# Reordering a planned kernel: new due times and transfer rules for a Fourier filter followed by a gated convolution

## Chip, cores and metric

The kernel runs on one NeuronCore of a Trainium2 chip. The metric is the device time of one execution in microseconds (us); the median of several executions counts. The engines are named as in the profile: PE is TensorE (matrix products), PEld its weight loads, DVE is VectorE, ACT is ScalarE, POOL is GpSimd, SP is SyncE, which here issues nearly all DMA transfers. SPq is SP's queue.

## What is computed

The input x has 8 batches of 3200 positions with 256 channels. Each batch is Fourier transformed along its positions, mixed by a complex matrix, soft-thresholded, and transformed back; a causal convolution of the result over five positions then gates a linear map of it, and a second linear map follows.

```python
X = np.fft.rfft(x, axis=1)
Yr = Xr @ w_r - Xi @ w_i + b_r
Yi = Xr @ w_i + Xi @ w_r + b_i
Yr = np.sign(Yr) * np.maximum(np.abs(Yr) - 0.01, 0.0)   # Yi likewise
y = np.fft.irfft(Yr + 1j * Yi, n=3200, axis=1)
gate_pre = sum(conv_w[k] * shifted(y, k) for k in range(5))
out = (sigmoid(gate_pre) * (y @ w_val)) @ w_out
```

## The kernel before

The transform of length 3200 = 64 x 50 is done in two stages, so that each batch goes through three parts.

**P1** (`p1`, and `p1_first` for batch 0): in 8 pieces a batch, x is loaded (two transfers of 200 KB), PE multiplies it with the 50-point transform f1 (tile p, line 499), ACT copies the result to s, and SP stores it to a buffer in HBM, a_dram.

**P2** (`p2`): in 13 steps u a batch, two frequency groups each (one in the last). SP loads a from a_dram. PE transforms it over 64 points with f2 (tile s, line 538, called s2 in the code). ACT and DVE split s into a high and a low half, xs (lines 548 and 550), and ACT adds a negated copy (553). PE mixes with w_r and w_i in y_ps, 12 products for each group (lines 573 and 574). DVE adds the bias (yb, 589), ACT and DVE do the threshold (tp, 594 and 596), both split the result into r_hl (293 and 295), and PE transforms it back over 64 points in z_ps (621). ACT copies that to z_t, which SP stores to z_dram.

**P3** (`positions` and `gated`): in 8 blocks k a batch, SP loads zl from z_dram, PE makes the inverse 50-point transform y_p (675), ACT copies it to y_sb. From y_sb come the product with w_val in v_ps (707, from a split y_hl; 703 for late blocks, from y_sb and the unsplit weights w_late) and the convolution: one ACT step (733) and four taps for each half of the channels on DVE (acc, 736), eight taps a block. ACT applies the sigmoid (746), DVE multiplies by v_ps (748) and splits the product (gated, 295), PE multiplies by w_out in o_ps (707), ACT copies it to o, and SP writes it out.

Before the first P3 of batch 0, DVE converts w_val, conv_w and w_out from 64-bit floating point (`from_float64`, lines 321 and 327: 13 steps for each matrix).

The three parts of neighbouring batches overlap: while batch b is in P2, batch b+1 is in P1 and batch b-1 in P3. What stands where is not written out by hand. Every piece of work is given to the class `Plan` by `add`, with a due time `at`, an engine, an estimated duration and the tiles that it uses and makes. `at` is counted in steps of P2 (13 a batch), shifted by the table `O`. `Plan.order` then walks through a model of the engines: on each, of the pieces that could begin within `SLACK` ns of the first, it takes the one with the lowest due time; it keeps one estimate, `wire`, of when the DMA engines are free; and it adds `LAND` ns after a piece before another engine may use its result. `SWITCH` prices a change on PE between the products of P1 and of y_p, which use a quarter of the array each (`quarters`), and the others. The kernel's instructions are issued in the order that results, each engine's in its own row; on the chip an engine takes its row strictly in that order, and only dependences set the time. `SLOTS` limits the buffers: one PSUM tile for each of s, y_ps and z_ps, two for p, y_p, v_ps and o_ps together, three buffers of x, a and zl.

The last two batches use some cheaper forms (`LATE_VAL`, `LATE_OUT`, `LATE_P2`): without a split, in full 32-bit products, which take PE longer and DVE and ACT shorter.

Of the kernel before, what the change touches and what calls it, by code (L numbers as in the profile page):

```python
# [79 lines left out]
class Plan:  # L80
# [30 lines left out]
    def order(self):  # L111
# [24 lines left out]
        free = {e: 0.0 for e in engines}  # L136
        in_quarters, wire = False, 0.0
# [13 lines left out]
        while len(done) < len(pieces):  # L151
            best = None
            for e in engines:
                could = []
                for p in waiting[e]:
                    at = opens(p)
                    if at is not None:
                        could.append((max(free[e], p["ready"], at), p))
                if not could:
                    continue  # L160
                first = min(c[0] for c in could)
                near = [c for c in could if c[0] <= first + SLACK[e]]
                start, p = min(near, key=lambda c: (c[1]["at"] - (TOGETHER if e == "PE" and in_quarters and c[1]["quarters"] else 0.0), c[0]))
                if best is None or start < best[0]:
                    best = start, p
            assert best is not None, "no piece can begin"
            start, p = best
            e = p["engine"]
            waiting[e].remove(p)
            busy, delay = p["busy"], p["delay"]  # L170
            if e == "PE":
                slow = max([f for until, f in CLOCK if start < until], default=1.0)
                busy, delay = busy * slow, delay * slow
                if in_quarters != p["quarters"]:
                    busy, delay = busy + SWITCH, delay + SWITCH
                in_quarters = p["quarters"]
            if p["kb"]:
                wire = max(wire, start + 800) + p["kb"] * 1024 / WIRE
                delay = wire - start + 1400
            free[e] = start + busy  # L180
            end = start + delay
            p["start"], p["end"] = start, end
            done.append(p)
            for t, tag in p["new"].items():
                rows[tag].append(t)
            for t in p["tiles"]:
                if t in users:
                    users[t] -= 1
                    ends[t] = max(ends[t], end)
            for n, at in [(n, end) for n in after[p["n"]]] + [(n, start) for n in follow[p["n"]]]:  # L190
                q = pieces[n]
                q["left"] -= 1
                q["ready"] = max(q["ready"], at)
                if not q["left"]:
                    waiting[q["engine"]].append(q)
# [22 lines left out]
def act(n, kind="copy"):  # L218
# [3 lines left out]

NU = (NT + 1) // 2
T = float(NU)
O = {
    "load_x": -1.5, "p1": -0.28, "p1_step": 1.25, "load_a": -2.0, "s2": -0.6, "s1i": 0.4,
    "p3": 2.6, "load_z": -2.0, "y": 0.2, "conv": 0.3, "val": 0.5, "gate": 0.9, "project": 1.2,
}
# [5 lines left out]

LATE = [(b, k) for b in (B - 2, B - 1) for k in range(NB)]
LATE_P2 = {(B - 1, NU - 2)}
LATE_VAL = set(LATE[5:])
LATE_OUT = set(LATE[15:])


@with_exitstack
def fourier_filter_then_gated_conv(ctx: ExitStack, tc: tile.TileContext, x, w_r, w_i, b_r, b_i,
# [3 lines left out]
    sb = ctx.enter_context(tc.tile_pool(name="sb", bufs=2))  # L246
    ps = ctx.enter_context(tc.tile_pool(name="ps", bufs=1, space=bass.MemoryType.PSUM))
    dram = ctx.enter_context(tc.tile_pool(name="dram", bufs=2, space=bass.MemoryType.DRAM))
    plan = Plan(SLOTS)
    add = plan.add  # L250
    tl = {}
# [233 lines left out]
    def p1(b, u, at):  # L485
# [20 lines left out]
        def store():  # L506
# [4 lines left out]
            for k in range(2):  # L511
                lo = u * 4 * D + k * 512
                nc.sync.dma_start(out=dst[:, :, lo:lo + 512], in_=st[k * HP:k * HP + N2])
        add(at + O["load_x"] + (b == 1), "SP", 700, load, STORED if b == 1 else (), [kx + (0,)], {kx: "x"}, kb=400, chain="x")
# [5 lines left out]
    def p2(b, u, at):  # L520
# [16 lines left out]
            for c in range(2):  # L537
                nc.tensor.matmul(p[:, 2 * i + c, :], tl[ka][:, i, c * P:(c + 1) * P], f2_sb[:, t, :], start=True, stop=True)  # L538
# [65 lines left out]
        kz, ko, kd = ("z_ps", bu), ("z_t", bu), ("z_dram", b)  # L604
# [46 lines left out]
    def positions(b, k, at):  # L651
# [28 lines left out]
        add(at, "PE", 900, s2i, [kz + (0,), ("g2", 0, 0), *free], [kp + (0,)], {kp: "ps_2"}, quarters=True, chain="s2i")  # L680
# [146 lines left out]

    def p1_all(b):
        for u in range(8):
            p1(b, u, (b - 1) * T + O["p1"] + u * O["p1_step"])  # L830
    for b in range(B):
        if b < B - 1:
            p1_all(b + 1)
# [8 lines left out]
        start = (b + 1) * T + O["p3"]  # L842
# [31 lines left out]
```

## Time and profile before

| | before |
|---|---|
| three runs | 994.38, 990.14, 991.02 us; median 991.02 us |
| profiled execution | 995.47 us, span 993.7 us |
| mean granted clock of TensorE | 0.963 |
| instructions | 23846, of them 9918 matmuls on PE |
| moved by DMA | 164.53 MB, mean 166 GB/s |

The span is the time from the first to the last instruction; the profiled execution's own time is 1.8 us longer. Busy time of PE counts the time in which at least one matmul is in flight. A full 32-bit product of the program appears as two records of matmul in the profile (256 rows of p in the program are 512 records). A row of the chain of waits has a start, a duration and what it was.

### The profile page before, as it was taken

What the parts mean: (1) busy time and instruction counts of PE and PEld (TensorE: products, weight loads), DVE (VectorE), ACT (ScalarE), POOL (GpSimd) and SP (SyncE); (2) the same over time, 40 slices, a digit from 0 to 9 for tenths busy, and PEclk for the clock granted to TensorE, in tenths of its full rate; (3) what the DMA queues carried; (4) which work ended last, traced back from release to release, by engine and by line L of the source; (5) the groups of instructions that cost most, each with busy time, mean ns of one, the idle gap of its engine ahead of it and who ended that gap; (6) DMA issues with size and microseconds to landing.
All of it is one profiled execution on the core that took longest, in us unless ns stands there. A gap on an engine that the chain in (4) does not pass through costs nothing.

```text
span 993.7 us, 23846 instructions
## 1 busy us (share of the span) xinstructions
PE 928.2 (93%) x9918; PEld 822.0 (83%) x9918; DVE 745.3 (75%) x1211; ACT 671.8 (68%) x1091; POOL 3.7 (0%) x8
## 2 busy tenths in 40 slices
PE   7699779999999999999999999999999899998896
PEld 2477648999898988899989998998988899996664
DVE  1244655979678886888797897889777798897775
ACT  1265446777677787678787787768686777775554
POOL 0000000000000000000000000000000000000000
PEclk8799959999999999999999999999999999999799
DMA  6688466443665357544665366635655245323321
GB/s 213 212 266 266 134 186 205 135 126 125 217 201 190 120 154 268 189 150 130 222 203 173 120 212 217 205 115 163 205 184 174 67 135 184 103 92 105 122 67 67
DMA packets 105233, 164.53 MB, mean 166 GB/s; under 512 B 10054, under 2 KB 78406, under 8 KB 105126
## 3 DMA queue, kind: packets, MB, share of 16 engines
q1 hardware_dynamic: 104166, 159.74, 50.3%
q10 hardware_dynamic: 960, 3.28, 0.9%
q8 instruction: 78, 1.28, 0.5%
q14 instruction: 29, 0.24, 0.1%
HBM read 84.34 MB, written 78.64 MB: 164 GB/s over the span
## 4 chain that ended last, share of the span: by engine, by line
PE 55%; DVE 29%; ACT 8%; DMA 4%; issue 2%; SPq 1%; ACTq 0%; DVEq 0%
DVE acc L736 15%; PE y_ps L573 10%; PE y_ps L574 10%; PE o_ps L707 8%; PE s L538 6%; PE v_ps L707 6%; PE z_ps L621 5%; PE p L499 4%; PE y_p L675 4%; DVE yb L589 2%; DVE acc L748 2%; DVE y_hl L295 2%; DVE xs L550 2%; ACT y_sb L682 2%; DMA x<-in_x 2%
## 5 line engine op out<-in xcount | busy, mean ns | idle before, releaser
L573 PE MATMUL y_ps<-wri_sb,xs 128*128 128x256 f32 x1200 | 299.6, 288 | 7.2 <-DVE yb L589 6.6
L736 DVE SCALAR_TENSOR_TENSOR acc<-y_sb,cw_sb,acc 128x400 f32<-128x400 f32 x512 | 297.7, 629 | 8.9 <-ACT acc L733 7.9
L574 PE MATMUL y_ps<-wri_sb,xs 128*128 128x256 f32 x1152 | 282.9, 284 | 1.4 <-ACT xs L553 0.8
L573 PEld LDWEIGHTS y_ps<-wri_sb,xs 128*128 128x128 f32 x1200 | 231.7, 193 | 19.9 <-issue 13.5
L574 PEld LDWEIGHTS y_ps<-wri_sb,xs 128*128 128x128 f32 x1152 | 221.6, 192 | 2.9 <-ACT xs L553 1.9
L707 PE MATMUL o_ps<-gated,wo_sb 128*128 128x400 f32 x756 | 157.7, 355 | 8.0 <-ACT gated L293 3.3
L707 PEld LDWEIGHTS o_ps<-gated,wo_sb 128*128 128x128 f32 x756 | 135.9, 192 | 14.1 <-ACT gated L293 4.7
L538 PE MATMUL s<-f_sb,a 128*128 128x128 f32 x800 | 117.9, 286 | 19.3 <-DVE xs L550 10.7
L538 PEld LDWEIGHTS s<-f_sb,a 128*128 128x128 f32 x800 | 105.8, 198 | 31.8 <-DVE xs L550 20.6
L707 PE MATMUL v_ps<-y_hl,wv_sb 128*128 128x400 f32 x636 | 128.1, 348 | 0.2 <-ACT y_sb L682 0.2
L594 ACT ACTIVATE tp<-yb,nlam 128x512 f32<-128x512 f32 (+1 forms) x103 | 72.8, 707 | 70.0 <-DVE yb L589 68.7
L589 DVE TENSOR_TENSOR yb<-y_ps,bias_sb 128x512 f32<-128x512 f32 (+1 forms) x103 | 68.5, 665 | 61.1 <-PE y_ps L574 60.9
L707 PEld LDWEIGHTS v_ps<-y_hl,wv_sb 128*128 128x128 f32 x636 | 112.5, 188 | 1.0 <-ACT y_sb L682 0.6
L746 ACT ACTIVATE acc<-acc 128x400 f32<-128x400 f32 x128 | 67.1, 538 | 49.6 <-DVE acc L736 49.0
L621 PE MATMUL z_ps<-r_hl,g_sb 128*128 128x256 f32 x594 | 95.4, 293 | 5.4 <-DVE r_hl L295 2.7
L621 PEld LDWEIGHTS z_ps<-r_hl,g_sb 128*128 128x128 f32 x594 | 80.4, 190 | 23.3 <-issue 6.5
L596 DVE SCALAR_TENSOR_TENSOR tp<-yb,tp 128x512 f32<-128x512 f32 (+1 forms) x103 | 69.0, 670 | 27.6 <-ACT tp L594 27.6
L550 DVE TENSOR_TENSOR xs<-s,xs 128x512 fp32r<-128x512 f32 (+1 forms) x104 | 69.0, 664 | 23.7 <-ACT xs L548 23.5
L295 DVE TENSOR_TENSOR r_hl<-tp,r_hl 128x512 fp32r<-128x512 f32 (+1 forms) x103 | 68.5, 665 | 23.9 <-ACT r_hl L293 22.8
L548 ACT CAST xs<-s 128x512 fp32r<-128x512 f32 (+1 forms) x104 | 58.7, 565 | 38.1 <-PE s L538 37.9
L733 ACT ACTIVATE acc<-y_sb,cw_sb 128x400 f32<-128x400 f32 x128 | 75.6, 630 | 5.4 <-DVE gated L295 5.4
L675 PEld LDWEIGHTS y_p<-g_sb,zl 50*64 50x64 f32 x4096 | 67.3, 137 | 14.0 <-issue 4.1
(70 smaller groups left out, 946.3 us busy)
## 6 DMA issues: line engine op xcount, KB each, us to landing
zl<-z_dram SPq DMA_DIRECT2D x128, 200.0 KB
out<-o SPq DMA_DIRECT2D x63, 400.0 KB
a<-a_dram SPq DMA_DIRECT2D x96, 256.0 KB
z_dram<-z_t SPq DMA_DIRECT2D x96, 256.0 KB
x<-in_x SPq DMA_DIRECT2D x120, 200.0 KB
a_dram<-s SPq DMA_DIRECT2D x120, 200.0 KB
x<-in_x ACTq DMA_DIRECT2D x8, 200.0 KB
f_sb<-in_f SPq DMA_DIRECT2D x5, 320.0 KB
```

The costliest lines, as they stand in the source:

```text
L295: add(at + 0.001, "DVE", dve(n), lambda: nc.vector.tensor_tensor(out=low(), in0=src(), in1=f32(high()), op=ALU.subtract), [*uses, hl[0]], ...
L538: nc.tensor.matmul(p[:, 2 * i + c, :], tl[ka][:, i, c * P:(c + 1) * P], f2_sb[:, t, :], start=True, stop=True)
L550: add(at + O["s2"] + 0.1, "DVE", dve(m * P), lambda: nc.vector.tensor_tensor(out=xs()[:, 0:m, 1, N1:], in0=tl[k2][:, 0:m, :], in1=f32(xs() ...
L573: nc.tensor.matmul(p[:, i, :], xr, wri_sb[:, 0, hw, c, :], start=k == 0, stop=False)
L574: nc.tensor.matmul(p[:, i, :], xi, wri_sb[:, 1, hw, c, :], start=False, stop=k == 5 and not late)
L589: nc.vector.tensor_tensor(out=buffer(kb, "yb", [P, 2, D])[:, 0:n], in0=tl[ky][:, 0:n], in1=b_, op=ALU.add)
L594: nc.scalar.activation(out=buffer(kt, "tp", [P, 2, D])[:, 0:n], in_=src()[:, 0:n], func=AF.Relu, bias=nlam)
L621: nc.tensor.matmul(p[:, i, :], g1_sb[:, hg, t, :], tl[kr][:, hr, i, :], start=k == 0, stop=k == 2)
L675: nc.tensor.matmul(pv[h][e * HP:(e + 1) * HP, c, m, :], zt[half(h), m, c * P + e * HP:c * P + (e + 1) * HP], g2_sb[half(h), :], start=True ...
L707: nc.tensor.matmul(p[:, e, 0:TB], w[:, hw, c, e * P:(e + 1) * P], src(hy, c), start=n == 0, stop=n == 5)
L733: nc.scalar.mul(block(acc(c)), y_at(k, c, 0), cw_sb[:, c, 0:1])
L736: nc.vector.scalar_tensor_tensor(out=block(acc(c)), in0=y_at(k, c, j), scalar=cw_sb[:, c, j:j + 1], in1=block(acc(c)), op0=ALU.mult, op1=A ...
```

## The change

The operations are the same; the order on every engine is new. In `Plan.order` a piece that issues a transfer can now be taken only when the modelled backlog of the wire is under `BACKLOG` = 5000 ns, and a result that PE takes from another engine is ready `WEIGHTS` = 130 ns later. `LAND` after PE goes from 150 to 215, `SWITCH` from 93 to 88, `WIRE` from 220 to 230, and the estimates for s2 and for the inverse 50-point transform change from 450 to 400 and from 900 to 950. All due times in `O` are new. By them P2's loads stand 3.8 steps ahead of the mix instead of 2.0, and its first product 2.3 instead of 0.6; P1 begins 1.5 steps later and its pieces stand closer; the third part begins 0.45 steps later, with its product w_out 4.1 steps behind a block's place instead of 1.2. The sets of late blocks stay as they were.

```diff
-                        could.append((max(free[e], p["ready"], at), p))
+                        could.append((max(free[e], p["ready"], at, wire - BACKLOG if p["kb"] else 0.0), p))
...
+                if q["engine"] == "PE" != e and at == end:
+                    at += WEIGHTS
...
-LAND = {"PE": 150, "DVE": 130, "ACT": 150, "POOL": 200, "SP": 0}
+LAND = {"PE": 215, "DVE": 130, "ACT": 150, "POOL": 200, "SP": 0}
...
-SWITCH = 93
+SWITCH = 88
+WEIGHTS = 130
...
-WIRE = 220
+WIRE = 230
+BACKLOG = 5000
...
-    "load_x": -1.5, "p1": -0.28, "p1_step": 1.25, "load_a": -2.0, "s2": -0.6, "s1i": 0.4,
-    "p3": 2.6, "load_z": -2.0, "y": 0.2, "conv": 0.3, "val": 0.5, "gate": 0.9, "project": 1.2,
-}
+O = {'load_x': -2.458,
+ 'p1': 1.206,
+ 'p1_step': 0.918,
+ 'load_a': -3.836,
+ 's2': -2.333,
...
+ 'project': 4.088,
...
-            add(at + O["s2"], "PE", 450, lambda i=i, t=t: s2(i, t), [ka + (0,), ("f2", t // 5, 0)], [k2 + (i,)],
+            add(at + O["s2"], "PE", 400, lambda i=i, t=t: s2(i, t), [ka + (0,), ("f2", t // 5, 0)], [k2 + (i,)],
```

Three places of the new order. First SP's row, near the end of the first part of batch 1: from the last load of a for batch 0 (the one with 128x256) to the first loads of a for batch 1. in_x is the input, and the store named s_894 is the last of P1 for batch 1. Before:

```order
L531 DMA a<-a_dram 128x256
L413 DMA g_sb<-in_g 50x50 x2
L427 DMA st_cw<-in_moe_conv_w 128x5x1 x2
L493 DMA x<-in_x 50x1024 x2
L634 DMA z_dram<-z_t 128x2x256 x2
L513 DMA a_dram<-s_894 100x1x512 x2
L493 DMA x<-in_x 50x1024 x2
L634 DMA z_dram<-z_t 128x2x256
L493 DMA x<-in_x 50x1024 x2
L513 DMA a_dram<-s_937 100x1x512 x2
L634 DMA z_dram<-z_t 128x2x256
L360 DMA st_1048<-in_moe_w_out 128x2x256
```

Behind these stands a row of three loads of a for batch 1. The same place after; the store named s_862 is the last of P1 for batch 1:

```order
L531 DMA a_dram<-s_862 100x1x512 x2
L431 DMA g_sb<-in_g 50x50 x2
L445 DMA st_cw<-in_moe_conv_w 128x5x1 x2
L549 DMA a<-a_dram 128x256
L652 DMA z_dram<-z_t 128x2x256 x2
L511 DMA x<-in_x 50x1024 x2
L549 DMA a<-a_dram 128x2x256 x2
L378 DMA st_975<-in_moe_w_out 128x2x256
L652 DMA z_dram<-z_t 128x2x256
L549 DMA a<-a_dram 128x2x256
```

The last store of P1 now stands ahead of batch 0's last load, and two loads of a for batch 1 stand ahead of w_out and of one store of z_t; a store of batch 2's first part is gone from this place.

Second DVE's row, in the second part of batch 6, around the split of s (xs) of the same step. Before:

```order
L295 TENSOR_TENSOR r_hl<-tp,r_hl 128x512
L295 TENSOR_TENSOR y_hl<-y_sb,y_hl 128x800
L736 SCALAR_TENSOR_TENSOR acc<-y_sb,cw_sb,acc 128x400 x8
L550 TENSOR_TENSOR xs<-s_9569,xs 128x4x128
L295 TENSOR_TENSOR y_hl<-y_sb,y_hl 128x800
L736 SCALAR_TENSOR_TENSOR acc<-y_sb,cw_sb,acc 128x400 x2
```

And after:

```order
L313 TENSOR_TENSOR r_hl<-tp,r_hl 128x512
L313 TENSOR_TENSOR y_hl<-y_sb,y_hl 128x800
L754 SCALAR_TENSOR_TENSOR acc<-y_sb,cw_sb,acc 128x400 x3
L766 TENSOR_TENSOR acc<-v_ps,acc 128x800
L754 SCALAR_TENSOR_TENSOR acc<-y_sb,cw_sb,acc 128x400 x3
L313 TENSOR_TENSOR gated<-acc,gated 128x800
L568 TENSOR_TENSOR xs<-s_9273,xs 128x4x128
```

Eight taps in one run stand ahead of the split before; after, six with two other steps between them. In the whole row, runs of exactly eight taps go from eleven to one.

Third PE's row, at the end of the program, from the last row of the last mix (y_ps with xz) on. Before:

```order
L574 MATMUL y_ps<-wri_sb,xz 128x256
L675 MATMUL y_p<-g_sb,zl 64x50 x32
L703 MATMUL v_ps<-y_sb,w_late 128x400 x2
L621 MATMUL z_ps<-r_hl,g_sb 128x256 x3
L703 MATMUL v_ps<-y_sb,w_late 128x400 x6
L707 MATMUL o_ps<-gated,wo_sb 128x400 x12
L675 MATMUL y_p<-g_sb,zl 64x50 x64
L707 MATMUL o_ps<-gated,wo_sb 128x400 x12
L703 MATMUL v_ps<-y_sb,w_late 128x400 x4
```

And after:

```order
L592 MATMUL y_ps<-wri_sb,xz 128x256
L725 MATMUL o_ps<-gated,wo_sb 128x400 x12
L721 MATMUL v_ps<-y_sb,w_late 128x400 x4
L639 MATMUL z_ps<-r_hl,g_sb 128x256 x3
L725 MATMUL o_ps<-gated,wo_sb 128x400 x12
L721 MATMUL v_ps<-y_sb,w_late 128x400 x4
L725 MATMUL o_ps<-gated,wo_sb 128x400 x12
L721 MATMUL v_ps<-y_sb,w_late 128x400 x4
L725 MATMUL o_ps<-gated,wo_sb 128x400 x12
L693 MATMUL y_p<-g_sb,zl 64x50 x96
```

More products of the blocks of batch 6 stand behind the last mix than before. From that row to the end, o_ps has 108 rows by wo_sb before and 144 after, v_ps by w_late 40 and 44, y_p 288 and 256.

More of the change, by code (lines that the diff above doesn't have):

```diff
@@ L224 @@
 T = float(NU)
-O = {
-    "load_x": -1.5, "p1": -0.28, "p1_step": 1.25, "load_a": -2.0, "s2": -0.6, "s1i": 0.4,
-    "p3": 2.6, "load_z": -2.0, "y": 0.2, "conv": 0.3, "val": 0.5, "gate": 0.9, "project": 1.2,
-}
+O = {'load_x': -2.458,
[3 more added lines that the diff above has]
+ 's2': -2.333,
+ 's1i': 0.635,
+ 'p3': 3.054,
+ 'load_z': -0.892,
+ 'y': 0.638,
+ 'conv': 1.077,
+ 'val': 1.65,
+ 'gate': -2.455,
+ 'project': 4.088,
+ 'late_val': 5,
+ 'late_out': 15,
+ 'p1_1': 0.0,
+ 'load_x_1': 1.0,
+ 'p1_2': 0.0,
+ 'p3_0': 0.0}
 WARM = 2, 1, 1, 1, 6
@@ L236 @@
 LATE_P2 = {(B - 1, NU - 2)}
-LATE_VAL = set(LATE[5:])
-LATE_OUT = set(LATE[15:])
 @with_exitstack
@@ L248, in fourier_filter_then_gated_conv @@
     dram = ctx.enter_context(tc.tile_pool(name="dram", bufs=2, space=bass.MemoryType.DRAM))
+    LATE_VAL, LATE_OUT = set(LATE[int(O["late_val"]):]), set(LATE[int(O["late_out"]):])
     plan = Plan(SLOTS)
@@ L513, in store @@
                 nc.sync.dma_start(out=dst[:, :, lo:lo + 512], in_=st[k * HP:k * HP + N2])
-        add(at + O["load_x"] + (b == 1), "SP", 700, load, STORED if b == 1 else (), [kx + (0,)], {kx: "x"}, kb=400, chain="x")
+        add(at + O["load_x"] + O["load_x_1"] * (b == 1), "SP", 700, load, STORED if b == 1 else (), [kx + (0,)], {kx: "x"}, kb=400, chain="x")
         add(at, "PE", 870, products, [kx + (0,), ("f1", 0, 0)], [kp + (0,)], {kp: "ps_2"}, quarters=True)
@@ L679, in positions @@
         free = [("turn", "read", (b - 1, j)) for j in range(4)] if k == NB - 1 and b else []
-        add(at, "PE", 900, s2i, [kz + (0,), ("g2", 0, 0), *free], [kp + (0,)], {kp: "ps_2"}, quarters=True, chain="s2i")
+        add(at, "PE", 950, s2i, [kz + (0,), ("g2", 0, 0), *free], [kp + (0,)], {kp: "ps_2"}, quarters=True, chain="s2i")
         lo = (k * MB + H0) * N2
@@ L829, in p1_all @@
         for u in range(8):
-            p1(b, u, (b - 1) * T + O["p1"] + u * O["p1_step"])
+            p1(b, u, (b - 1) * T + O["p1"] + O.get(f"p1_{b}", 0.0) + u * O["p1_step"])
     for b in range(B):
@@ L841, in fourier_filter_then_gated_conv @@
                 later_constants(u)
-        start = (b + 1) * T + O["p3"]
+        start = (b + 1) * T + O["p3"] + O.get(f"p3_{b}", 0.0)
         for i, k in enumerate([NB - 1] + list(range(NB))):
```

## The prediction

> **What bounds the kernel now.** I read the page first: which engine is full, and when.
>
> ```profile
> span 993.7 us, 23846 instructions
> PE 928.2 (93%) x9918; PEld 822.0 (83%) x9918; DVE 745.3 (75%) x1211; ACT 671.8 (68%) x1091; POOL 3.7 (0%) x8
> ...
> PE   7699779999999999999999999999999899998896
> ...
> PEclk8799959999999999999999999999999999999799
> ```
>
> TensorE (PE) is the engine that counts; it is short of full at the start, at the end and around slices 28 and 31, and the granted clock (PEclk) falls at much the same places. An order can win nothing where PE is full, so I next cut the span into stretches: the head (to 161 us, where the first product of the third part starts), the body to 905 us, where the last mix ends, and the tail. Columns are stretch, length, busy time of PE, PEld, DVE, ACT, POOL, then granted clock, DMA share and GB/s.
>
> ```profile
> 80.00:103.00 23.00, 21.02 (x159) 17.59 (x156) 10.34 (x15) 12.52 (x21) 0.00 (x0) 0.93 0.80 246
> 103.00:161.00 58.00, 44.78 (x301) 35.23 (x303) 33.27 (x70) 26.69 (x44) 0.00 (x0) 0.79 0.56 171
> 161.00:250.00 89.00, 84.94 (x1035) 79.12 (x1027) 77.39 (x128) 67.45 (x112) 0.00 (x0) 1.00 0.45 140
> 250.00:410.00 160.00, 158.65 (x1838) 144.84 (x1841) 126.24 (x204) 121.09 (x196) 0.00 (x0) 1.00 0.58 189
> 410.00:676.00 266.00, 262.02 (x3042) 244.57 (x3035) 219.76 (x355) 202.04 (x330) 0.00 (x0) 1.00 0.55 175
> 676.00:800.00 124.00, 117.27 (x1280) 108.32 (x1279) 99.43 (x158) 89.55 (x147) 3.01 (x2) 0.97 0.50 158
> 800.00:905.00 105.00, 104.33 (x1140) 100.93 (x1139) 89.04 (x146) 76.91 (x130) 0.00 (x0) 1.00 0.39 124
> 905.00:993.70 88.70, 71.16 (x782) 50.66 (x781) 64.69 (x106) 44.57 (x72) 0.00 (x0) 0.89 0.28 93
> ```
>
> The two rows of the chain that set the cuts at 161 and 905 us (start, duration, what):
>
> ```profile
> 160.68 1.08 PE y_p L675 x64
> ...
> 905.68 0.12 PE y_ps L574
> ```
>
> A stretch loses time in two ways. It is idle: length less PE busy. And a granted clock of 0.79 leaves about 1 - 0.79 of the stretch's work undone. From 80 to 161 us: idle 2.0 + 13.2 = 15.2, clock 0.07 x 23 + 0.21 x 58 = 13.8; together 29 us of 81. From 161 to 905 us: idle 4.1 + 1.3 + 4.0 + 6.7 + 0.7 = 16.8, clock 0.03 x 124 = 3.7; together 20.5 us of 744. In the tail PE idles 88.7 - 71.2 = 17.5 us and DVE, with 64.7 us, is the busier one for its length.
>
> **Part A, the head: 80 to 161 us.** The chain of waits and the timeline show three things. First, after the last store of the next batch's first part, SyncE's queue (SPq) reaches that batch's loads only much later:
>
> ```profile
> 107.37 1.62 SPq L513 DMA_DIRECT2D a_dram<-s  x2
> ...
> 121.28 0.39 SPq L634 DMA_DIRECT2D z_dram<-z_t  x1
> 121.77 0.41 SPq L360 DMA_DIRECT2D st<-in_moe_w_out  x1
> 122.23 1.52 SPq L531 DMA_DIRECT2D a<-a_dram  x3
> ```
>
> The loads of a stand behind a store of z_t (121.28), which waited for the second part's own chain. Second, VectorE (DVE) converts w_val in one run, 13 steps, followed by the small one of conv_w, and the bias of a finished mix stands behind both; PE waits for it (columns: total, times, longest):
>
> ```profile
> 116.11 2.14 DVE L321 TENSOR_SCALAR st<-st 128x512 int32<-128x512 int32 x5
> ...
> 122.80 0.86 DVE L321 TENSOR_SCALAR st_cw<-st_cw 128x10 int32<-128x10 int32 x5
> ...
> 125.10 0.68 DVE L589 TENSOR_TENSOR yb<-y_ps,bias_sb 128x512 f32<-128x512 f32 x1
> ```
>
> ```profile
> PE y_ps L573 <- DVE yb L589: 5.6, 1, 5.6
> PE s L538 <- DVE xs L550: 3.4, 2, 2.0
> ```
>
> Third, the clock stays low for most of what follows. In the new order (SP and PE rows) the loads of a for batch 1 stand ahead of w_out and of the store that waits, four products of P1 of batch 2 with their transfers come later, and s of a step is a whole mix ahead of its use. The conversions stay. The run of w_val itself lasts 122.80 - 116.11 = 6.7 us, and I keep the 5.6 us that it costs now, since the new order has no more to put beside it. I keep half of the clock's loss (6.9) with it, and 4.5 us for the start of batch 1, whose second conversion remains as well. That is 17 of 29: **gain 12 us**. The ends: 0, if the idle time only moves; 20, if nothing stays but the 5.6 and about 3.4 of clock.
>
> **Part B, the body: 161 to 905 us.** Here the largest wait that PE shows by itself is for DVE's low half of xs, and one example shows why:
>
> ```profile
> PE s L538 <- DVE xs L550: 6.6, 10, 2.9
> ```
>
> ```profile
> 781.41 4.45 DVE L736 SCALAR_TENSOR_TENSOR acc<-y_sb,cw_sb,acc 128x400 f32<-128x400 f32 x8
> 785.78 0.68 DVE L550 TENSOR_TENSOR xs<-s,xs 128x512 fp32r<-128x512 f32 x1
> ```
>
> ```profile
> 783.60:786.50 2.90, 0.04 (x1) 0.00 (x0) 2.90 (x7) 2.55 (x5) 0.00 (x0) 1.00 0.20 68
> 786.50:791.00 4.50, 4.48 (x25) 4.48 (x26) 4.50 (x7) 3.07 (x6) 0.00 (x0) 0.62 0.22 62
> ```
>
> Eight taps of the convolution stand in a row on DVE, the subtraction that frees s's PSUM tile stands behind them, and PE is empty for 2.9 us; then the clock is at 0.62 for 4.5 us, another 1.7 us. The order before has eleven such runs of eight, the order after has one; runs of two to six, with the steps of P2 between them, take their place. The price of what could go is 6.6 of idle and 3.7 of clock, 10.3 us. I take **gain 6 us**, since DVE is still busy 612 of 744 us in these rows (77.4 + 126.2 + 219.8 + 99.4 + 89.0) and some waits will only move. Ends: a loss of 10, if as large a wait of another kind appears, and a gain of 20, all that is lost. The 12 fewer changes on PE between the small tiles of P1 and the inverse transform and the large ones are counted at nothing; no row prices one.
>
> [...]
>
> **Part C, the tail: after the last mix.** "P2 far ahead" shows in the count of rows that PE still has after its last mix. Before: 108 rows of o_ps, 40 of v_ps by w_late, 288 of y_p. After: 144, 44, 256. So three more blocks' products with w_out and one more with w_val wait until then, and one inverse transform fewer. The chain of waits prices them (start, duration, what):
>
> ```profile
> 881.33 4.37 DVE acc L736 x8
> ...
> 891.82 2.19 PE o_ps L707 x12
> ...
> 914.18 0.90 DVE acc L748
> ...
> 916.72 0.91 DVE gated L295
> ...
> 928.40 2.69 PE v_ps L703 x8
> 931.09 1.12 PE y_p L675 x64
> ```
>
> A v_ps of four rows in the order is eight records here, a y_p of 32 rows 64. So 3 x 2.19 + 2.69 - 1.12 = 8.1 us of PE work leaves the stretch where PE is full and goes to one where it idles 17.5 us. That is worth 8.1 us only if the tail grows by nothing, and the tail's length is DVE's. DVE's steps after the last r_hl: before 80 taps, 10 of L748, 9 of gated; after 78, 11 and 10. At 4.37/8 = 0.546, 0.90 and 0.91: 43.7 + 9.0 + 8.2 = 60.9 against 42.6 + 9.9 + 9.1 = 61.6, so 0.7 us more. The cover is PE's idle time; if it is gone, all 8.1 come back. DVE idles 88.7 - 64.7 = 24 us in that stretch, much of it at the turn of the last batch; the new order there is regular (five taps, L748, three taps, gated) and I give it 0.6 us. **Gain 8 us.** Ends: 0, and 17 if the regular order also saves some 9 of those 24.
>
> **The sum.** 12 + 6 + 8 = 26 us. The profiled execution took 995.5 us, of it a span of 993.7; by it the new one takes 969.5. The median of the three timed runs is 991.02, 4.5 lower, and the forecast is for that: 991 - 26 = **965 us**.
>
> **The rivals.**
>
> *The clock stays low* (17%). The conversion on DVE still empties PE for over 5 us and the steps after it are still short of work, so that the head stays at 0.79 and A gives 2 instead of 12. For it: both conversions stay in DVE's rows. Against: b1's loads come earlier. Then 991 - 2 - 6 - 8 = 975 us.
>
> *Everything comes at once* (12%). A reaches 20, B 12, C 12: 947 us. For it: the planner's new allowances for what follows a product on PE are longer, 215 instead of 150 ns, which spaces dependent steps all over the body.
>
> *No change* (10%). The order's table says where a transfer stands, not when the wire is free; if the head's idle time only moves (A 0), the body's waits are replaced (B 0) and the tail grows with its products so that C is 2, the time is 989 us. For it: most of the body is at 98% already (262.02 of 266).
>
> *Slower: P2 overtakes its data* (13%). One step of the plan is a thirteenth of a batch, and a batch takes 109.7 us, as these two rows of the chain at the same place in two batches show; a step is 8.4 us.
>
> ```profile
> 552.02 2.27 DVE acc L736 x4
> ...
> 661.71 2.27 DVE acc L736 x4
> ```
>
> By the tables, the last product of P1 for a batch stands 2.5 steps (21 us) ahead of that batch's first load of a before, and 1.5 steps (13 us) after. Between them lie the copy and the store, and the load follows. In the crowded head the chain shows what these take:
>
> ```profile
> 22.80 5.53 DMA a_dram<-s
> ...
> 41.44 8.53 DMA a<-a_dram
> ```
>
> With a product and a copy of about 1 us each that is 16 us, 3 more than 13. If the wire is as slow in the body, s stands in PE's order before its data is there, and PE, in order, waits 3.1 us at each of 7 batches and loses 1.7 us of clock each time, as at 786 us: 7 x 4.8 = 34 us, A and B give nothing, C 8: 991 + 34 - 8 = 1017 us. With A and B at nothing it decides the sign from 8/7 = 1.1 us per batch on. Against: DMA is at 0.50 to 0.58 in the body, 0.80 in the head, and s stands 2.3 steps ahead of its mix, so the planner has placed it with room. [...]
>
> **How the numbers follow.** The forecast has 48%, with 957 to 974 for its own bounds. A measurement of this kernel can tell about 0.5%, 5 us, from no change. Faster: 48 + 17 + 12 = 77%, and the clock's rival belongs there; same 10%; slower 13%. The range leaves out the slow case and about half of the best: 946 to 992.
>
> **What would show it.** Right: from 80 to about 150 us the clock above 0.9 and PE idle for less than 8 us except beside L339; no PE wait above 2 us behind a run of taps in the body; the last mix ending some 26 us earlier and the stretch after it not longer than 89 us. Wrong: waits of s on a at each batch; a tail of more than 95 us; a head as long as before, with the first y_p at 160 us.

## The result and the profile after

| | before | after |
|---|---|---|
| median of the runs compared | 990.58 us (989.82 to 994.38, four) | 937.89 us (937.06 to 938.41, four) |
| ratio, with its 95% interval | | 0.946 (0.9434 to 0.9486) |
| profiled execution, span | 995.47 us, 993.7 us | 938.27 us, 936.5 us |
| mean granted clock | 0.963 | 0.985 |

The new order is 5.4% faster, 52.7 us by the medians and 57.2 us by the two profiled executions. The stretches below are those of these two executions; that of the kernel before was slower than all four runs of the table, so some 4.5 us of the difference in them need not be the order's. The forecast was 965 us with a range from 946: the sign was right, the gain was twice the 26 us forecast, and the time lies 8 us under the range.

The page of the new kernel, with its busy times, PE by slices and the granted clock by slices:

```profile
span 936.5 us, 23789 instructions
PE 901.2 (96%) x9918; PEld 806.0 (86%) x9918; DVE 739.3 (79%) x1211; ACT 671.5 (72%) x1091; POOL 3.7 (0%) x8
...
PE   7799699999999999999999999999999999999897
...
PEclk9699899999999999999999999999999999999999
```

Counted from 0, PE's row has no digit below 9 from slice 5 to slice 36, where before slice 5 was at 7 and slices 31 and 36 were at 8 (the prediction names 28 and 31, but slice 28 is at 9), and the clock's row has none below 9 after the head. PE is busy 27.0 us less with the same 9918 matmuls, so part of what counted as busy before was lost time, some of it at a lower clock. The stretches by the same marks as before (the start of the first y_p, the end of the last mix) are 141.0 and 857.2 us; the columns are those of the prediction's rows. Before:

```profile
0.00:160.60 160.60, 129.43 (x801) 93.15 (x801) 68.74 (x119) 69.82 (x109) 0.67 (x6) 0.85 0.68 213
160.60:905.80 745.20, 728.41 (x8347) 678.86 (x8349) 611.86 (x986) 557.46 (x912) 3.01 (x2) 1.00 0.51 164
905.80:993.70 87.90, 70.36 (x775) 49.99 (x775) 64.69 (x106) 44.56 (x71) 0.00 (x0) 0.89 0.28 92
```

And after:

```profile
0.00:141.00 141.00, 119.43 (x789) 88.52 (x789) 69.01 (x120) 67.15 (x107) 0.67 (x6) 0.90 0.70 217
141.00:857.20 716.20, 712.33 (x8381) 665.47 (x8381) 602.17 (x980) 556.54 (x909) 3.07 (x2) 1.00 0.55 174
857.20:936.50 79.30, 69.44 (x755) 52.00 (x753) 68.14 (x112) 47.77 (x77) 0.00 (x0) 1.00 0.34 115
```

The head is 19.6 us shorter, the body 29.0 and the tail 8.6: all of the 57.2. PE's idle time (length less PE busy) goes from 31.2 to 21.6 in the head, from 16.8 to 3.9 in the body and from 17.5 to 9.9 in the tail. The finer cuts, for the part of the head that the prediction speaks of and for the length of the body:

```profile
80.00:103.00 23.00, 22.73 (x186) 19.54 (x184) 13.27 (x22) 15.08 (x25) 0.00 (x0) 1.00 0.71 216
103.00:144.00 41.00, 31.76 (x296) 27.72 (x297) 30.43 (x67) 21.96 (x38) 0.00 (x0) 0.92 0.69 200
144.00:234.00 90.00, 88.21 (x1048) 82.23 (x1047) 77.42 (x125) 72.80 (x122) 0.00 (x0) 1.00 0.59 188
...
390.00:640.00 250.00, 249.69 (x2846) 232.66 (x2839) 208.43 (x347) 192.27 (x314) 0.00 (x0) 1.00 0.56 179
640.00:760.00 120.00, 118.51 (x1435) 110.78 (x1434) 101.17 (x162) 95.04 (x157) 3.07 (x2) 1.00 0.52 170
```

After 144 us PE idles 1.8 us in the first stretch shown, 0.3 of 250 us in the middle and 1.5 between 640 and 760 us, with a clock of 1.00 in all. What PE still waits for (total, times, longest), in the head from 80 to 144 us:

```profile
PE y_ps L592 <- ACT xs L571: 5.9, 1, 5.9
PE s L556 <- DVE xs L568: 2.1, 2, 1.4
```

and in the body, where the largest wait is this:

```profile
PE s L556 <- DVE xs L568: 1.3, 1, 1.3
PE v_ps L725 <- ACT r_hl L311: 0.7, 1, 0.7
```

The wait of s for xs fell from 6.6 us in ten pieces to one of 1.3. The wait of 5.9 us in the head is the old one of 5.6 us behind the conversion of w_val on DVE, under another name: the split of s (xs) now stands behind the conversion's last step, where the bias stood before. DVE's row (start, duration, what):

```profile
101.58 2.14 DVE L339 TENSOR_SCALAR st<-st 128x512 int32<-128x512 int32 x5
...
107.66 0.69 DVE L345 TENSOR_TENSOR st<-st 128x512 f32<-128x512 f32 x1
108.27 0.68 DVE L568 TENSOR_TENSOR xs<-s,xs 128x512 fp32r<-128x512 f32 x1
```

SP's queue, at the place that the prediction showed for before:

```profile
98.59 1.60 SPq L531 DMA_DIRECT2D a_dram<-s  x2
...
105.42 0.93 SPq L549 DMA_DIRECT2D a<-a_dram  x2
106.46 0.39 SPq L378 DMA_DIRECT2D st<-in_moe_w_out  x1
```

Batch 1's first loads of a are issued 6.8 us after the last store of its P1 (105.42 - 98.59), where before it was 14.9 us (122.23 - 107.37).

### The profile page after: what moved, and what is told of

The parts are those of the page before. It is cut to its first block, busy times and chain, and to the rows that moved or that the text cites. A ratio compares the mean times of both kernels' runs of the same rounds, so it can differ in the third digit from the quotient of the medians.

```text
span 936.5 us, 23789 instructions
## 1 busy us (share of the span) xinstructions
PE 901.2 (96%) x9918; PEld 806.0 (86%) x9918; DVE 739.3 (79%) x1211; ACT 671.5 (72%) x1091; POOL 3.7 (0%) x8
## 4 chain that ended last, share of the span: by engine, by line
PE 67%; DVE 21%; ACT 5%; DMA 4%; issue 2%; SPq 1%; ACTq 0%; DVEq 0%
PE y_ps L591 12%; PE y_ps L592 12%; DVE acc L754 10%; PE o_ps L725 10%; PE v_ps L725 9%; PE s L556 8%; PE z_ps L639 7%; PE y_p L693 5%; PE p L517 5%; DVE acc L766 2%; DVE gated L313 2%; DVE yb L607 2%; DMA x<-in_x 1%; DVE xs L568 1%; DVE y_hl L313 1%
## 5 line engine op out<-in xcount | busy, mean ns | idle before, releaser
L591 PE MATMUL y_ps<-wri_sb,xs 128*128 128x256 f32 x1200 | 296.4, 287 | 2.0 <-DVE yb L607 1.2
L592 PE MATMUL y_ps<-wri_sb,xs 128*128 128x256 f32 x1152 | 277.5, 281 | 5.9 <-ACT xs L571 5.9
L591 PEld LDWEIGHTS y_ps<-wri_sb,xs 128*128 128x128 f32 x1200 | 227.4, 189 | 11.0 <-issue 5.9
L592 PEld LDWEIGHTS y_ps<-wri_sb,xs 128*128 128x128 f32 x1152 | 218.9, 190 | 6.1 <-ACT xs L571 6.1
L725 PE MATMUL o_ps<-gated,wo_sb 128*128 128x400 f32 x756 | 151.2, 348 | 0.0
L556 PEld LDWEIGHTS s<-f_sb,a 128*128 128x128 f32 x800 | 101.8, 193 | 26.1 <-DVE xs L568 11.6
L556 PE MATMUL s<-f_sb,a 128*128 128x128 f32 x800 | 112.1, 282 | 9.0 <-DVE xs L568 4.8
L612 ACT ACTIVATE tp<-yb,nlam 128x512 f32<-128x512 f32 (+1 forms) x103 | 72.5, 705 | 23.3 <-DVE yb L607 20.9
L311 ACT CAST gated<-acc 128x800 fp32r<-128x800 f32 x63 | 54.3, 862 | 45.3 <-DVE acc L766 45.1
L614 DVE SCALAR_TENSOR_TENSOR tp<-yb,tp 128x512 f32<-128x512 f32 (+1 forms) x103 | 68.6, 666 | 18.6 <-ACT tp L612 18.5
```

The source lines that it names most:

```text
L591: nc.tensor.matmul(p[:, i, :], xr, wri_sb[:, 0, hw, c, :], start=k == 0, stop=False)
L592: nc.tensor.matmul(p[:, i, :], xi, wri_sb[:, 1, hw, c, :], start=False, stop=k == 5 and not late)
L612: nc.scalar.activation(out=buffer(kt, "tp", [P, 2, D])[:, 0:n], in_=src()[:, 0:n], func=AF.Relu, bias=nlam)
L614: add(at + 0.2, "DVE", dve(n * D), lambda: nc.vector.scalar_tensor_tensor(out=tl[kt][:, 0:n], in0=src()[:, 0:n], scalar=LAM, in1=tl[kt][:, ...
L725: nc.tensor.matmul(p[:, e, 0:TB], w[:, hw, c, e * P:(e + 1) * P], src(hy, c), start=n == 0, stop=n == 5)
```

## The experiments

The theory to be tested: the due times make the gain, by giving each result more room before PE needs it. The rivals: the planner's rules and constants make it; the broken runs of eight taps make it; the late products with w_out are only moved work. Twelve kernels took parts out of the new kernel or changed one in it (E1 to E6, E8), or put parts into the old one (E7, E9 to E12). Each edit is to the planner, so the rest of the order shifts with it.

In the table, head, body and tail are cut at the two marks from above. "Lost" is the length of a stretch less its matmul records at the pace that they keep in runs without a wait, in us a record from start to start: y_ps 0.117, s 0.111, z_ps 0.118, p 0.121, y_p 0.0164, v_ps and o_ps 0.1825, 0.336 for the late 32-bit form, and 0.43 for the 22 warm-up products of the head. So work that moves across a mark does not count in it. What is left as lost is not all to be won: the changes from one kind of product to another are in it (in the new kernel p starts 0.20 us after the last y_ps ahead of it, at 118.46 and 118.26 us, where y_ps keeps 0.117 by itself). The last column counts the rows of o_ps by wo_sb behind the last mix (the 148 of E10's expectation has four rows by w_late more). The stretches come from one profiled execution of each kernel, which lies up to 7.0 us from its median (E4).

| kernel | median, us | ratio (95%) | head, body, tail | lost in them | o_ps |
|---|---|---|---|---|---|
| before | 990.58 | 1 | 160.6, 745.2, 87.9 | 60.0, 39.1, 28.9 | 108 |
| after | 937.89 | 0.946 (0.9434 to 0.9486) | 141.0, 716.2, 79.3 | 42.3, 16.2, 12.2 | 144 |
| E1 after, old table | 984.66 | 0.9922 (0.9894 to 0.9949) | 155.9, 741.9, 84.8 | 49.2, 40.5, 27.1 | 108 |
| E2 after, old constants | 944.28 | 0.9522 (0.9491 to 0.9553) | 143.5, 717.4, 79.1 | 44.9, 17.4, 12.0 | 144 |
| E3 after, no backlog rule | 947.46 | 0.9543 (0.9517 to 0.9569) | 154.8, 713.2, 78.7 | 52.3, 17.0, 11.6 | 144 |
| E4 after, P2 near | 952.44 | 0.9611 (0.957 to 0.9652) | 153.6, 726.8, 77.3 | 53.5, 25.9, 12.5 | 132 |
| E5 after, taps in one run | 960.74 | 0.9696 (0.9663 to 0.9729) | 141.1, 737.7, 83.4 | 42.4, 35.3, 18.6 | 132 |
| E6 after, w_out early | 948.79 | 0.9566 (0.9539 to 0.9593) | 141.7, 722.4, 83.8 | 43.1, 20.1, 19.0 | 132 |
| E7 before, taps spread | 991.34 | 1.0003 (0.999 to 1.0016) | 160.4, 743.7, 85.2 | 59.8, 35.9, 27.9 | 120 |
| E8 after, conversion split | 941.67 | 0.95 (0.9477 to 0.9524) | 149.9, 712.5, 78.7 | 45.0, 18.8, 11.6 | 144 |
| E9 before, P2 far | 965.01 | 0.972 (0.9673 to 0.9767) | 151.0, 733.8, 81.6 | 53.2, 25.8, 21.7 | 120 |
| E10 before, blocks late | 967.43 | 0.9754 (0.9717 to 0.9791) | 161.0, 725.1, 79.0 | 60.3, 27.1, 11.8 | 144 |
| E11 before, both | 953.87 | 0.9622 (0.9588 to 0.9656) | 148.9, 723.7, 80.0 | 51.1, 22.8, 12.9 | 144 |
| E12 before, whole table | 949.77 | 0.9586 (0.9551 to 0.9621) | 147.0, 720.4, 80.1 | 49.2, 19.6, 13.0 | 144 |

Differences between kernels are taken below from the ratios, times 990.6 us, since each set of runs had its own runs of before.

**E1: the new rules with the old table.**

```diff
-O = {'load_x': -2.458,
- 'p1': 1.206,
- 'p1_step': 0.918,
- 'load_a': -3.836,
- 's2': -2.333,
...
+O = {
+    "load_x": -1.5, "p1": -0.28, "p1_step": 1.25, "load_a": -2.0, "s2": -0.6, "s1i": 0.4,
+    "p3": 2.6, "load_z": -2.0, "y": 0.2, "conv": 0.3, "val": 0.5, "gate": 0.9, "project": 1.2,
+    "late_val": 5, "late_out": 15, "load_x_1": 1.0,
+}
```

> The kernel after with the due times of before (the whole table O), all rules and constants of the model as after. Theory D (the due times make the gain: they break up DVE's runs of taps and bring the last mix forward): runs of exactly eight taps are back (12), o_ps behind the last mix is back at 108 rows, so 970 to 992 us, with PE idle 15 us or more in the body. Rival M (the recalibrated model, with more time after PE and ahead of PE, makes it): 938 to 950 us.

Of the 53.5 us (0.054 x 990.6) the rules alone give 7.7 (0.0078 x 990.6). Body and tail lose what they lost before (40.5 and 27.1). So most of the gain is the due times'; E12 below measures them without the rules.

**E2: the new table with the old constants.**

```diff
-LAND = {"PE": 215, "DVE": 130, "ACT": 150, "POOL": 200, "SP": 0}
+LAND = {"PE": 150, "DVE": 130, "ACT": 150, "POOL": 200, "SP": 0}
-SWITCH = 88
-WEIGHTS = 130
+SWITCH = 93
+WEIGHTS = 0
-WIRE = 230
+WIRE = 220
```

The estimates of 400 and 950 ns go back to 450 and 900 as well.

> The kernel after with the old constants of the model (150, 93, 220, no extra time ahead of PE, 450 and 900 for the two products), new due times and the backlog rule kept. Theory D: the counts behind the last mix (144, 44, 256) and the runs of taps stay, so 936 to 948 us. Rival M: PE's dependent steps stand too close again, idle 10 us or more in the body, 955 to 985 us.

The constants are worth 6.1 us (0.0062 x 990.6); the profiled spans differ by less, 3.6 us, most of it in the head, since the profiled execution was the fastest of this kernel (941.86 us, the median is 944.28). That the longer allowances space the steps of the whole body, the reason of the rival "everything at once", is not seen: the body loses 17.4 us without them and 16.2 with them.

**E3: no limit on the wire's backlog.**

```diff
-BACKLOG = 5000
+BACKLOG = 10 ** 9
```

> The kernel after without the rule on the wire's backlog. Rival T (the head's gain of 20 us is the transfer rule's: without it four products of P1 for batch 2 stand ahead of the first y_p again, 92 rows of p instead of 76): the first y_p at 152 to 160 us and 950 to 958 us in all. Theory D: the head keeps its place, because loads of a stand early by their due times: first y_p within 6 us of 141, 936 to 945 us.

The transfer rule is worth 8.2 us, and all of it lies in the head (lost 52.3 against 42.3; the body and the tail are as after). Without it, PE waits in the stretch from 80 to 160 us mostly for a copy of P1's product:

```profile
PE p L517 <- ACT s L522: 7.4, 3, 6.2
PE z_ps L639 <- DVE r_hl L313: 4.1, 1, 4.1
```

Before 80 us it also waits longer for a load of a, 7.3 us against 3.6 in the new kernel:

```profile
PE s L556 <- DMA a<-a_dram: 7.3, 1, 7.3
```

**E4: the new kernel with P2 near again.**

```diff
- 'load_a': -3.836,
- 's2': -2.333,
+ 'load_a': -2.0,
+ 's2': -0.6,
```

> The kernel after with P2's load and first product at the old due times (2.0 and 0.6 steps ahead of the mix instead of 3.8 and 2.3). Theory D in its first form (P2's lead is what frees PE): PE waits for s and xs again, 8 us or more in the body, and the time is 955 to 980 us. In its second form (the late products of the blocks do it, since they fill PE while P2's chain runs): 938 to 950 us; one block of o_ps fewer behind the last mix costs 2 us of that.

P2's lead is worth 15.0 us here; the time lies between the two cases expected. The profiled execution was the slowest of this kernel, 959.46 us against 951.58 to 952.88 for the other three. In it the head loses 11.2 us more than in the new kernel (53.5 - 42.3) and the body 9.7 (25.9 - 16.2); where the 7 us lie by which it is slower than the median is not known. Its largest wait, 6.6 us in the head, has no releaser in the profile, but DVE's and PE's rows show what it is: the split of s stands behind the conversions of w_val and conv_w, and s starts as the split ends. So it is the wait of 5.9 us of the new kernel in another place.

```profile
109.42 0.69 DVE L345 TENSOR_TENSOR st<-st 128x512 f32<-128x512 f32 x1
...
113.40 0.68 DVE L568 TENSOR_TENSOR xs<-s,xs 128x512 fp32r<-128x512 f32 x1
```

```profile
114.18 2.05 PE L556 MATMUL s<-f_sb,a 128*128 128x128 f32 x8 [6.62 <-issue]
```

In the body the waits are many and small, and the wait of s for xs is not back, as the first form of the theory had it:

```profile
PE y_ps L591 <- DVE yb L607: 2.2, 7, 0.4
...
PE s L556 <- DVE xs L568: 1.2, 2, 0.7
```

**E5: the eight taps of a block as one piece.**

```diff
-        for j in range(1, KC):
-            for c in range(2):
-                add(at + O["conv"] + 0.02 * j, "DVE", dve(TB), lambda c=c, j=j: tap(c, j), ...
+        def taps():
+            for j in range(1, KC):
+                for c in range(2):
+                    tap(c, j)
+        add(at + O["conv"] + 0.02, "DVE", 8 * dve(TB), taps, [*here, *there], ...
```

> The kernel after with the eight taps of a block given to the planner as one piece, so that 62 runs of exactly eight stand on DVE's row (1 in the kernel after); due times and rules as after. Theory R (the runs of taps, with P2's steps behind them, are what PE waits for in the body): body idle back to 10 us or more, body 724 to 738 us instead of 716, in all 948 to 962 us. Rival N (runs are harmless where P2's products stand 2.3 steps ahead of their mix): body within 5 us of 716, 938 to 944 us.

With 62 runs of eight taps instead of one, the kernel is 23.4 us slower, and 21.5 of it lie in the body. The waits are no longer those of before: y_p waits for a PSUM tile that DVE frees late, and s for xs only 2.3 us in the body. The body's row and its waits:

```profile
141.10:878.80 737.70, 724.06 (x8392) 669.85 (x8392) 605.95 (x983) 553.34 (x913) 2.98 (x2) 0.99 0.53 170
```

```profile
PE y_p L693 <- DVE acc L768: 4.6, 8, 1.7
PE z_ps L639 <- DVE r_hl L313: 2.6, 2, 2.3
PE s L556 <- DVE xs L568: 2.3, 5, 1.0
```

PE's idle time rose by only 9.7 us (13.6 against 3.9) where the stretch grew by 21.5; the other 11.7 (724.06 - 712.33) count as busy. Of those, 12 rows of o_ps that left the tail are 2.2 us. So whole runs do cost much in this order (R).

**E6: the product with w_out early again.**

```diff
- 'project': 4.088,
+ 'project': 1.2,
```

> The kernel after with the product by w_out due 1.2 steps behind a block's place as before, instead of 4.1. Theory L (late products of the blocks are PE's spare work, with which it fills the time that P2's chain takes): body idle 9 us or more and 950 to 965 us. Rival P (P2's lead does that alone): 938 to 946 us, of it about 2 us for one block of o_ps fewer behind the last mix.

10.5 us slower, between the two cases expected: the body is 6.2 us longer, of which 2.2 is one block's product that moved back into it, and the tail 4.5 us longer although it holds that product less. The body's idle time did not rise, 2.6 us against 3.9, so the mechanism as I stated it, that late products fill PE's gaps in the body, is not what was seen there. In the tail PE idles 11.9 us against 9.9, and the clock is at 0.96:

```profile
864.10:947.90 83.80, 71.86 (x744) 51.01 (x742) 68.06 (x112) 47.00 (x76) 0.00 (x0) 0.96 0.31 104
```

**E7: the old kernel with the taps' due times spread.**

```diff
-                add(at + O["conv"] + 0.02 * j, "DVE", dve(TB), lambda c=c, j=j: tap(c, j), ...
+                add(at + O["conv"] + 0.12 * j, "DVE", dve(TB), lambda c=c, j=j: tap(c, j), ...
```

> The kernel before with the due times of a block's taps spread (0.12 steps for each instead of 0.02); nothing else. Runs of exactly eight taps go from 11 to 5. Theory R: the body loses some of its 16.8 us of idle time, 978 to 986 us, of it 1 to 2 us for one block of o_ps more behind the last mix. Rival N: 987 to 995 us.

Five runs of eight are left of eleven, and nothing is gained in the time; the body is 1.5 us shorter and loses 3.2 us less. In the body s still waits for xs, a little less, and z_ps now waits for r_hl, the next step of the same kind (before: 6.6 and 1.9 us):

```profile
PE s L538 <- DVE xs L550: 5.2, 9, 1.4
PE z_ps L621 <- DVE r_hl L295: 4.0, 6, 1.2
```

So the runs of taps alone are not what bound the old body; to break six of the eleven gains nothing there.

**E8: the new kernel with the conversion of w_val split.** Its 13 steps wait in three pieces of five, five and three for steps of P2 of batch 0 (its due time stays).

```diff
-            add(at + 0.0001 * k, "DVE", busy, piece, uses, done, new if k == 0 else None, ...
+            add(at + 0.0001 * k, "DVE", busy, piece, [*uses, *(g for lo, g in gate if lo <= k)], done, ...
...
+            load_matrix64(7.1, "w_val", w_val, wv_sb, (), [(0, turn("low", 11)), (5, turn("yb", 11)),
+                          (5, turn("low", 12)), (10, turn("yb", 12))])
```

> The kernel after with the conversion of w_val split on DVE's row: five of its steps stand behind the split of s for step 11, five behind the bias of step 11, three behind that of step 12, where after has all 13 in one run ahead of the split for step 11. Theory C (that run is what empties PE for 5.9 us in the head and halves the clock for 6.8 us behind it): idle of 5.9 down to under 2, at most one window of half clock there, 928 to 934 us. Rival W (PE has nothing else to do in that place, since the first part's transfers are late, and another wait takes its place): 936 to 940 us.

4.0 us slower than the new kernel. The wait of 5.9 us is gone and three shorter ones stand in its place, in the stretch from 80 to 160 us:

```profile
PE y_ps L592 <- DVE xz L579: 2.9, 1, 2.9
PE s L556 <- DVE xs L568: 2.6, 1, 2.6
PE z_ps L639 <- ACT r_hl L311: 2.0, 1, 2.0
```

Together 7.5 us, against the 5.9 + 2.1 of the new kernel's head: the waiting only moved, and the body loses 18.8 us instead of 16.2. The clock's part hardly changed either: the new kernel is at 0.52 for the 6.8 us from 108.0 us on, behind its gap of 5.9, and E8 is at 0.52 from 117.0 to 120.5 us and at 0.50 from 141.0 to 144.4; that is 3.3 and 3.4 us of clock. That the conversion's run is the head's last limit (C) does not hold: split in this way, it costs time in this order.

**E9: the old kernel with P2 far ahead, and nothing else.**

```diff
-    "load_x": -1.5, "p1": -0.28, "p1_step": 1.25, "load_a": -2.0, "s2": -0.6, "s1i": 0.4,
+    "load_x": -1.5, "p1": -0.28, "p1_step": 1.25, "load_a": -3.836, "s2": -2.333, "s1i": 0.4,
```

> The kernel before with two due times of the new table alone: the loads of a at -3.836 and s2 at -2.333. Taking these two back out of the new kernel cost 14 us. If the parts of the table add up, this gains about 14: 977 us, 11 of it ahead of the first y_p and the rest in the body. If P2's lead needs the blocks' new times (runs of exactly eight taps go from 11 to 21 here, and each can hold up a split of s), it gains under 5 and the body gets longer than 745 us.

Two numbers give 27.7 us, half of the whole gain and twice the 14 us expected, though DVE's row has 21 runs of eight taps instead of eleven. The body is 11.4 us shorter, and s waits for xs there only this long:

```profile
PE s L538 <- DVE xs L550: 1.1, 2, 0.8
```

There are more long runs, and most of the wait behind them is gone. I read this so that with s 2.3 steps ahead of its mix instead of 0.6, PE has other rows to take while DVE finishes; no row shows that by itself.

**E10: the old kernel with the blocks' new times, P2 near.**

```diff
-    "load_x": -1.5, "p1": -0.28, "p1_step": 1.25, "load_a": -2.0, "s2": -0.6, "s1i": 0.4,
-    "p3": 2.6, "load_z": -2.0, "y": 0.2, "conv": 0.3, "val": 0.5, "gate": 0.9, "project": 1.2,
+    "load_x": -1.5, "p1": -0.28, "p1_step": 1.25, "load_a": -2.0, "s2": -0.6, "s1i": 0.635,
+    "p3": 3.054, "load_z": -0.892, "y": 0.638, "conv": 1.077, "val": 1.65, "gate": -2.455, "project": 4.088,
```

> The kernel before with only the block's due times of the new table (p3, load_z, y, conv, val, gate, project, and s1i), P2 near as before. No run of eight taps is left, and 148 rows of o_ps stand behind the last mix. If the parts add up, the body gains at least the 6 us that the late products gave back in the other direction, and the time is 979 us or less, with the head still near 160 us. If the blocks' times need P2's lead, under 3 us: 988 to 992.

24.4 us, nothing of it in the head (161.0 against 160.6), 20.1 in the body and 8.9 in the tail. In DVE's row no run of eight is left; in the body s waits 1.7 us for xs, and the wait of 4.3 us that p had for a PSUM tile freed by DVE's product with v_ps (L748) is no longer among the largest. Before, then E10:

```profile
PE p L499 <- DVE acc L748: 4.3, 6, 1.8
```

```profile
PE v_ps L707 <- ACT y_sb L682: 3.5, 5, 0.8
PE s L538 <- DVE xs L550: 1.7, 2, 1.4
```

So the wait for xs also goes with s as near to its mix as before.

**E11: both in the old kernel.** The edits of E9 and E10 together.

> The kernel before with both: P2 far ahead and the block's new times; P1's times and all rules of the planner as before. If the two parts add up, the gain is the sum of those measured for each alone. If they need each other, it is more than that sum by over 10 us. In either case a body near 716 us (as in the new kernel) says that the body's gain is these due times alone; one above 730 says that P1's times or the planner's rules have a share.

37.4 us, less than 27.7 + 24.4 = 52.1: neither expected case. The two do not need each other; they remove partly the same loss. The body's lost time shows it: 39.1 before, 25.8 and 27.1 with one of them, 22.8 with both. The body's length, 723.7 us, lies between the 716 and the 730 that were named.

**E12: the old kernel with the whole new table.** E11 and P1's times (load_x, p1, p1_step).

> The kernel before with the whole new table, old rules and constants. The rules with the old table gave 6 us. If table and rules add up, this takes 938 + 6 = 944 us, all of the difference in the head. If the rules only pay with the new table (each alone cost 6 and 10 us when taken out), 954 us, again all in the head. A body longer than 722 us speaks against both.

41.0 us; P1's times add 3.6. The rules add 12.5 us to this (0.0126 x 990.6) against 7.7 on the old table, between the two cases expected. Not all of it lies in the head as I expected: of 11.0 us between the profiled spans, 947.5 - 936.5, 6.0 are in the head and 4.2 in the body.

No kernel here was faster than the new one.

## Why the prediction was wrong in size

**Its sign and its places were right.** The forecast's marks for "right" came true: the clock is 1.00 and 0.92 from 80 to 144 us; PE's idle time there is 0.3 + 9.2 us, 3.6 us without the wait beside the conversion; no wait over 2 us stands behind taps in the body; the tail is 79.3 us, under 89. The last mix ends 48.6 us earlier instead of 26. None of the marks for "wrong" came.

**Part B is the step that failed.** The body is 29.0 us shorter; 8.1 of these are the products that part C had moved, and 20.9 stand against "I take gain 6 us". Two links of that step broke.

The first: "DVE is still busy 612 of 744 us in these rows" and "some waits will only move". DVE is as busy after, 602 of 716 us, and the waits did not move: PE's idle time fell from 16.8 to 3.9. So a DVE that is 84% busy had room here. Either of two remedies took the wait for xs away. P2's lead alone took it from 6.6 to 1.1 us while the long runs of taps became more (E9); the blocks' times alone took it to 1.7 us with P2 near (E10). Fewer runs alone gave nothing (E7). So the reason that I gave, eleven runs to one, was not sufficient for the gain, though whole runs would have spoilt it (E5, 23.4 us). That both remedies work by the distance from a step to its use is my reading of these edits; in the new kernel P2 near brings other waits, not that for xs (E4).

The second: I took idle time and clock, 16.8 + 3.7 = 20.5 us, as "all that is lost". PE's busy time in the body fell by 16.1 us (728.41 - 712.33); 8.1 of it moved to the tail, 1.9 came in from the head (its length less what it lost was 160.6 - 60.0 us and is 141.0 - 42.3), and 3.7 was clock, so that some 6 us were lost while records in flight kept PE "busy". By the pace of the records the body lost 39.1 us before and 16.2 after, a gain of 22.9. The bound was too low, since a matmul here is in flight longer than the next one waits to start: y_ps has a mean of 284 ns (L573) and a pace of 117.

```profile
L573 PE MATMUL y_ps<-wri_sb,xs 128*128 128x256 f32 x1012 | 247.4, 284 | 1.0 <-DVE yb L589 1.0
```

**Part A: the right mechanism, too small.** The 29 us lost from 80 to 161 us became 9.5 of idle and 0.08 x 41 = 3.3 of clock from 80 to 144 us, 12.8; a gain of 16 instead of 12, and 19.6 for the whole head. Of the 17 us that I kept, the conversion's wait is as it was put down, 5.9 against 5.6 us. The kept half of the clock's loss, 6.9, came out as 3.3, and the 4.5 for the start of batch 1 as 3.6 of idle. The "about 3.4 of clock" in A's upper end has no row beside it in the prediction; the traces have 6.7 us at 0.50 behind the gap of 5.6 us before (125.2 to 131.9 us), 3.4 us of clock, and 6.8 us at 0.52 behind the gap of 5.9 us after, 3.3. The rest of the head's gain lies before 80 us or at the mark itself. E3 and E9 show two causes: the transfer rule is worth 8.2 us, all in the head, and P2's lead alone shortens the old head by 9.6 us.

**Part C: right that the tail takes 8.1 us of PE work without growing, wrong that it would only just do so.** It shrank by 8.6 us, so that C is 16.7 against 8, near the end of 17 that I named. DVE is busy 3.5 us more in the stretch, where its counted steps gave 0.7, but it idles 11.2 us instead of 23.2 (79.30 - 68.14 and 87.90 - 64.69), where I gave the regular order 0.6 us. PE's waits in the tail before and after:

```profile
PE v_ps L703 <- DVE acc L748: 3.9, 2, 2.9
PE o_ps L707 <- ACT gated L293: 3.3, 3, 2.2
```

```profile
PE y_p L693 <- DVE acc L766: 1.7, 3, 0.8
PE y_p L693 <- issue: 1.3, 1, 1.3
```

E10 shows that the blocks' times are enough for this: with them alone the tail is 79.0 us. P2's lead alone takes it to 81.6 (E9).

**The rivals.** All three parts came out at or next to their upper ends, 20, 20 and 17, if A is given the whole head; that is "everything at once", to which I gave 12% and 947 us because I capped it at 20, 12 and 12. Its reason, the longer allowances, is not the main cause: all the constants together are worth 6.1 us (E2). "P2 overtakes its data" did not come: no wait of s for a is among those of the body, and in the head, where I took the price from, P2's lead gave 9.6 us instead of taking any, although s waits there 9.6 us for a in E9 against 8.2 before. Middles taken for three parts, each with a reason of its own for caution, left the joint upper case outside the range. The parts did not come out independently: each of the two groups of due times helps in the body and in the tail (E9, E10), so one cause may drive several parts; that it is room ahead of PE's use in all of them is argued, not shown.

**What stays open:** which of the blocks' eight times makes E10's gain (E6 prices w_out alone at 10.5 us in the new kernel), and how P2's lead and the blocks' times free PE in the body, since most of what they win there is spread over small waits and over time that counts as busy.

## What to carry to other kernels

In a row that an engine takes in the order given (before, DVE starts the split of s at 785.78 us, behind the eight taps that stand ahead of it in the row and start at 781.41), look at how far ahead of its use a result is made, before looking at what stands in front of it on the other engine: 1.7 steps more of distance gave 27.7 us here, and breaking six of the eleven long runs in front gave none. That does not make long runs harmless: to join all taps into runs of eight in the new order cost 23.4 us. Two remedies for the same loss do not add up, so test each alone and both together. And where the parts of a forecast may share a cause, their upper ends can come together, and the range should hold that case.

## What was not expected of the hardware

In these runs the length of a gap alone does not tell the clock after it. Before, after the gap of 5.6 us in the head, PE ran at about half speed twice, with a stretch of nearly full clock (0.93) between them (length, then PE busy, the last three numbers granted clock, DMA share and GB/s):

```profile
125.60:132.40 6.80, 5.07 (x21) 3.21 (x22) 3.69 (x9) 3.38 (x6) 0.00 (x0) 0.54 0.47 154
132.40:135.80 3.40, 1.40 (x9) 0.99 (x8) 3.10 (x8) 1.97 (x4) 0.00 (x0) 0.93 0.54 167
135.80:149.40 13.60, 12.15 (x53) 8.41 (x54) 5.74 (x10) 4.66 (x7) 0.00 (x0) 0.52 0.65 193
```

By the records that is a little over half the pace: y_ps starts every 0.213 us from 145.76 to 148.53 us, in the third row, against 0.117 at full clock. In that row PE is busy 12.15 of 13.6 us, with its last gap of more than 0.1 us ending at 141.2 us, some 8 us before the row ends, and still stays at 0.52, while the gap of 2.9 us at 786 us was followed by 0.62 for 4.5 us only. In E8, a stretch of 3.5 us in which PE is never idle has 0.52, though no gap of that kernel there was over 2.9 us:

```profile
117.00:120.50 3.50, 3.50 (x19) 3.50 (x18) 2.67 (x5) 0.86 (x2) 0.00 (x0) 0.52 0.64 215
```

No run here shows what sets the length of such a stretch.
